# Placing the moving and the stationary operand of 1296 matmuls at equal addresses modulo 512 bytes

## The chip, the core and the metric

The kernel runs on one core of one Trainium2 chip. The metric is device time in microseconds. Three runs of the kernel before gave 567.34, 567.60 and 567.75 us; the median, 567.6 us, is the time before. In the text, PE is TensorE, DVE is VectorE, ACT is ScalarE, POOL is GpSimd and SP is SyncE.

## The reference

Three layers follow each other: attention with a window, a mixture of experts, and a gated layer. The last one takes most of the time, and the change is made there.

```
x = attention(q, k, v)        # 2 batches, 8 heads, 768 positions, 64 wide -> 1536 tokens x 512
x = moe(x, w_gate, w_output_gate, w1, w2)       # 8 experts, 512 -> 1024 -> 512, one per token
gate = 1 / (1 + exp(-(x @ w_gate)))             # 1536 x 512 times 512 x 1536
val  = x @ w_val                                # the same shape
out  = (gate * val) @ w_out                     # 1536 x 1536 times 1536 x 512
```

The weights of the last layer come as 64-bit floats, and the kernel turns them to 32 bits itself.

## The kernel before, in words

**Split operands.** A product that must be better than one pass of the type float32r is made of three. Each operand x is split in a high part, `hi` (line 131, on ACT), and the rest, `lo` (line 134, on DVE or POOL): high by high, high by low and low by high are added in one PSUM bank.

**The experts (before 254 us).** Seven items of up to 256 tokens of one expert are computed. `item_A` (line 652) makes the hidden layer: the weights are the stationary operand (128x128), the tokens the moving one (256 columns). `item_B` (line 661) makes the output: the hidden layer `hh`, `hl` is stationary, the weights `w2h`, `w2l` move with 512 columns. All these tiles lie in the pools `mA2` and `mB`. A last, short item (lines 671 and 683) follows.

**Gate and value (254 to 457 us).** The tokens are transposed into `yb[b]`, three pairs (high and low) of tiles of 128 x 4 x 512, one pair for each block `b` of 512 tokens. `gate_val(f, b)` makes 12 matmuls for the gate in a PSUM bank of the tag A and 12 for the value in a bank of the tag B: four chunks `c` of the inner dimension by three products. Stationary is `wh` or `wl` (chunk c, 128x128, 512 bytes in each partition), moving is `yb[b]` (chunk c, 512 columns, 2048 bytes in each partition). ACT takes the sigmoid of the first bank (line 1145), DVE multiplies it with the second (line 1146, recorded at 137) into `gg`. The columns f run from 0 to 11, each with b = 0, 1, 2, except at the start, where f = 0 and 1 are mixed: (0,0), (1,0), (0,1), (0,2), (1,1), (1,2). Between the chunks DVE does the conversion of the next weights, seven operations each (lines 760 to 777), ACT and POOL split them.

**Output (457 to 558 us).** For each of 12 tiles of 128 tokens, 36 matmuls run (line 1176): `gs`, the split product of gate and value (128x128), is stationary; the split output weights move, 512 columns. These weights are written into the same tiles `yb`, which the tokens no longer need: `yb[0]` holds f = 0 to 3, `yb[1]` 4 to 7, `yb[2]` 8 to 11. DVE copies the bank out, POOL sends the rows with an indirect DMA (line 1179).

**What sets the order and the addresses.** The order is the order of the code on each engine. A tile's address is set by what was laid in the same side of the memory before it: pools on the left side count up from the low end in the order of the code, those on the right count down from the high end. `yb[0]` is the last tile but a few small ones in the pool `cp`, on the left; `wh` and `wl` lie in `wsp` and the four tiles `yr` in `yrp`, both on the right; `gs` lies in `d1`, on the right as well, below them.

The lines that the change and the prediction's steps touch are: the tiles of `cp` (163 to 182), the pools `yrp` and `wsp` (1046 to 1052), `gate_val` (1125 to 1146), `g_split` and `wo_split` (1110 to 1123), and the output loop (1169 to 1181).

Of the kernel before, what the change touches and what calls it, by code (L numbers as in the profile page):

```python
# [10 lines left out]
F32 = mybir.dt.float32  # L11
F32R = mybir.dt.float32r
# [96 lines left out]
def moe_kernel(tc, A, out):  # L109
# [4 lines left out]
    def pool(st, name, side=None, space=None):  # L114
        kw = dict(name=name, bufs=1, reuse_waits="tile")
        if side:
            kw["side"] = side
        if space is not None:
            kw["space"] = space
            kw.pop("reuse_waits")  # L120
        return st.enter_context(tc.tile_pool(**kw))

    cp = pool(top, "cp", "left")
# [39 lines left out]
    x_t = dp.tile([S, DM], F32, name="x_t")  # L163
    y_c = dp.tile([NTOK + SLOT, XW], F32, name="y_c")

    ck = cp.tile([128, 128], F32, name="ck")
    ident = cp.tile([128, 128], F32, name="ident")
    ckb = cp.tile([128, CKB], BF16, name="ckb")
    wgo = cp.tile([128, 4, 16], F32, name="wgo")
    lg = cp.tile([128, NT, 16], F32, name="lg")  # L170
    OH = cp.tile([128, NT, 8], BF16, name="OH")
    cum = cp.tile([128, B, 2, 8], BF16, name="cum")
# [6 lines left out]
    gidx = cp.tile([128, 18, 2], I32, name="gidx")  # L179
    gix = cp.tile([128, 2], I32, name="gix")  # L180
    row_id = cp.tile([128, 12], I32, name="row_id")
    yb = [[cp.tile([128, 4, 512], F32R, name=f"yb0{k}") for k in range(2)]]
    tri, ones = ckb[:, 0:128], ckb[:, 128:256]
    count, token = ckb[:, 256:256 + SLOT], ckb[:, 256 + SLOT:256 + SLOT + 2 * TB].rearrange("p (t k) -> p t k", k=2)
    k8e, ke = ck[:, 0:8], ck[:, 16:24]
# [447 lines left out]
    def split2(p):  # L633
        s = slice(2 * p, 2 * p + 2)
        hi(w2h[:, s], w2r[:, s])
        lo(w2l[:, s], w2r[:, s], w2h[:, s])
# [9 lines left out]
    def item_A(f):  # L646
        hp = bank("A", 3)[:, 0:SLOT]
        s = slice(f * 128, f * 128 + 128)
        n = 0
        for c in range(4):  # L650
            for w, x in ((w1h, xTh), (w1h, xTl), (w1l, xTh)):
                PE.matmul(hp, w[:, c, s], x[:, c], start=n == 0, stop=n == 11)  # L652
                n += 1
        SC.activation(out=hh[:, f], in_=hp, func=AF.Relu)
        V.scalar_tensor_tensor(out=hl[:, f], in0=hp, scalar=0.0, in1=hh[:, f].bitcast(F32), op0=ALU.max, op1=ALU.subtract)  # L655
# [7 lines left out]
    def last_item(yp):  # L663

        t = slice(0, 128)
        ht = [w1r[:, q] for q in range(2)]

        def part(q, hp, cs_):
            for c in cs_:
                for n, (x, w) in enumerate(((xTh, w1h), (xTl, w1h), (xTh, w1l))):  # L670
                    PE.matmul(hp, x[:, c, t], w[:, c, q * 512:q * 512 + 512], start=c == 0 and n == 0, stop=c == 3 and n == 2)

        def turn(q):
            tp = bank("B", 2).rearrange("p (g c) -> p g c", g=4)
            for g_ in range(4):
                PE.transpose(tp[:, g_], ht[q][:, g_ * 128:g_ * 128 + 128], ident)
            s = slice(4 * q, 4 * q + 4)
            hi(hh[:, s, t], tp)
            lo(hl[:, s, t], tp, hh[:, s, t])

        def second(f):
            for n, (x, w) in enumerate(((hh, w2h), (hh, w2l), (hl, w2h))):
                PE.matmul(yp[0], x[:, f, t], w[:, f], start=f == 0 and n == 0, stop=f == 7 and n == 2)

        split2(1)
        hp = bank("A", 3)
        part(0, hp, range(4))
        SC.activation(out=ht[0][:, 0:512], in_=hp, func=AF.Relu)
        hp = bank("A", 3)
        part(1, hp, range(2))  # L690
        turn(0)
        part(1, hp, range(2, 4))
        split2(2)
        SC.activation(out=ht[1][:, 0:512], in_=hp, func=AF.Relu)
        for f in range(2):
            second(f)
        turn(1)
        split2(3)
        for f in range(2, 8):
            second(f)  # L700
# [52 lines left out]
    def ypsum(i):  # L753
        t = ps.tile([128, 2, 512], F32, tag="C", bufs=1, name=f"yp{i}")
        return t[:, 0], t[:, 1]
# [34 lines left out]
    wsp = {}  # L790
# [29 lines left out]
    def run(g, n=1):  # L820
        for _ in range(n):
            next(g, None)

    with tc.manual_schedule():
# [186 lines left out]
        for i in range(NSTAT):  # L1011
            if i == 3:
                last = nc.values_load(itab[0:1, 1, 15:16], engines=(ET.SP, ET.DVE), min_val=NSTAT - 1, max_val=MAXI - 1, skip_runtime_bounds_check_because=SKIP)
            if i == NSTAT - 1:
                yp = ypsum(i)
                last_item(yp)
                break
            if i:
                for f in range(8):
                    item_A(f)  # L1020
                    if f % 2 == 0:
                        split2(f // 2)
                    elif i > 1:
                        run(bg, 1)
                    if i == 1:
                        if f in (1, 3, 4, 5):
                            run(tb, 1)
                        if f == 5:
                            item_regs(2)
                            item_gather(2, gidx[:, 2])  # L1030
            if i < NSTAT - 1:
                load_w(reg["e", i + 1], reg["e", i + 1] != reg["e", i], range(8) if i else range(4, 8))
            yp = ypsum(i)
            for f in range(8):
                item_B(f, yp)
                if f % 2 == 0 and i < NSTAT - 1:
                    split1(f // 2)
                if f in (4, 5) and (f == 4 or i < NSTAT - 2):
                    item_T(i + 1, f - 4)
                if i and f in ((1, 2, 3) if i == 1 else (1, 2, 3, 6)):  # L1040
                    run(bg, 1)
                if not i and f == 0:
                    run(g, 9)
                    tail_st.close()

                    yr_st = ExitStack()
                    yrp = pool(yr_st, "yrp", "right")
                    yrt = [yrp.tile([128, XW], F32, name=f"yr{k}") for k in range(4)]
                    for t in yrt:
                        G.memset(t, 0.0)  # L1050
                    ws_st = ExitStack()
                    wsp_ = pool(ws_st, "wsp", "right")
                    cv_st = ExitStack()
                    cv = pool(cv_st, "cv", "right")

                    todo = [("w", f, k) for f in range(2) for k in range(2)]
                    bg = background(todo)
                    for k in todo[:3]:
                        load_raw(k)
                if not i and f in (1, 3, 7):  # L1060
                    run(tb, 1)
                if i == 5 and f in (0, 2, 3, 6):
                    t = (0, 2, 3, 6).index(f)
                    y_T(t)
                    load_y(t + 4, few)
                if i == 5 and f == 7:
                    split2(0)
            if i < NSTAT - 1:
                item_out(i, yp, reg["c", i] if i else 0)
            if 0 < i < NSTAT - 2:  # L1070
                if i + 2 == NSTAT - 1:
                    V.tensor_copy(gix, gidx[:, bass.ds(last, 1)].rearrange("p o h -> p (o h)"))
                item_gather(i + 2, gix if i + 2 == NSTAT - 1 else gidx[:, i + 2], halves=1 if i + 2 == NSTAT - 1 else 2)
            for k in (() if i == 0 else (3, 4) if i == 1 else (i + 3,)):
                more(k)

            if i == 4:
                n_items = nc.values_load(itab[0:1, 0, 15:16], min_val=0, max_val=MAXI - 1, skip_runtime_bounds_check_because=SKIP)
                few = n_items < NSTAT
                for t in range(4):  # L1080
                    load_y(t, few)
# [30 lines left out]
        def g_split(t):  # L1112
            for k in range(2):
                gs[t, k] = d1.tile([128, 2, 6, 128], F32R, tag="gs", bufs=3, name=f"gs{t}{k}")
                src = gg[:, 6 * k:6 * k + 6, t * 128:t * 128 + 128]
                hi(gs[t, k][:, 0], src)
                lo(gs[t, k][:, 1], src, gs[t, k][:, 0])
# [38 lines left out]
        for f in range(2, 12):  # L1156
            if f == 11:
                run(bg, 999)
                cv_st.close()
                d1_st = ExitStack()  # L1160
                d1 = pool(d1_st, "d1", "right")
            for b in range(3):
                gate_val(f, b)
                if f == 11:
                    if b == 0:
                        g_split(0)
                    for w in range(4 * b, 4 * b + 4):
                        wo_split(w, G if w % 2 else None)
        for t in range(12):
# [12 lines left out]
        y_st.close()  # L1182
        g_st.close()
        d1_st.close()
        ws_st.close()
        yr_st.close()
    top.close()


# [57 lines left out]
```

## Time and profile before

| | us |
|---|---|
| median of three runs | 567.6 |
| the profiled execution, its own time | 565.83 |
| its span, first to last instruction | 564.0 |
| PE busy (matmuls) | 542.9 |
| DVE busy | 386.8 |
| ACT busy | 213.7 |
| POOL busy | 124.8 |
| line 1136, first to last matmul's start | 254.1 to 457.4 |
| line 1176, first to last matmul's start | 457.7 to 557.4 |

A matmul of 512 columns is shown as 394 ns long, but the next one starts long before it ends, so the busy times of single matmuls overlap. What a matmul costs in a row of them is the distance between starts: a group of 12 in the chain of waits takes some 2.8 us, which is 232 ns each. The numbers in the prediction are such distances.

### The profile page before, as it was taken

Reading aid. Unit: us, or ns where it says so; the run is one execution under the profiler, and the core shown is the slowest. Engines: PE = TensorE matmul, PEld = TensorE weight load, DVE = VectorE, ACT = ScalarE, POOL = GpSimd, SP = SyncE. Lnnn points to the kernel's source line nnn. Section 1 sums busy time; section 2 is a strip of 40 time slices with the busy share of each in tenths; the row PEclk is TensorE's granted clock in tenths of the full one; section 3 lists DMA queues with packets and bytes.
Section 4 is the critical chain, followed back from the end, with each engine's and each line's share of the span. In section 5 each row is a group of like instructions: output and inputs, shape, how many; then the busy total and the mean of one; then the engine's idle time right before and its main releaser. Section 6 shows DMA issues by size and latency. Waiting matters only on the chain.

```text
span 564.0 us, 8978 instructions
## 1 busy us (share of the span) xinstructions
PE 542.9 (96%) x3236; PEld 458.9 (81%) x3236; DVE 386.8 (69%) x735; ACT 213.7 (38%) x391; POOL 124.8 (22%) x151
## 2 busy tenths in 40 slices
PE   8899989989999999989999999999999999999995
PEld 4688979878989989868888888888888888888884
DVE  4777677879777687853778899999987763323320
ACT  2866774654546555643221212212111442112110
POOL 3673044173101100000011111111111152212211
PEclk9989999999999999999999999999999999999998
DMA  8991465962478403216132323323322000001010
GB/s 326 414 408 39 149 245 179 382 247 74 133 268 268 160 24 108 76 57 206 38 100 87 101 87 112 112 76 112 111 76 76 1 1 37 20 37 38 19 38 37
DMA packets 31983, 71.62 MB, mean 127 GB/s; under 512 B 3056, under 2 KB 11712, under 8 KB 31936
## 3 DMA queue, kind: packets, MB, share of 16 engines
q1 hardware_dynamic: 28816, 60.96, 30.9%
q0 software_dynamic: 3120, 10.06, 5.2%
q8 instruction: 26, 0.43, 0.3%
q14 instruction: 21, 0.17, 0.1%
HBM read 72.53 MB, written 11.33 MB: 149 GB/s over the span
## 4 chain that ended last, share of the span: by engine, by line
PE 34%; issue 15%; POOL 5%; ACT 0%; POOLq 0%; DVE 0%; DVEq 0%; ACTq 0%
PE ps_A L1136 18%; PE ps_B L1136 15%; POOL out_dram L1179 3%; POOL yb L134 1%; PE ps_B L746 1%; POOLq L1243 0%; ACT yb L131 0%; ACT gs L131 0%; DVE yt L141 0%; DVE gg L137 0%; POOLq L1179 0%; POOL yt L706 0%; POOLq L1084 0%; DVEq L137 0%; POOLq L134 0%
## 5 line engine op out<-in xcount | busy, mean ns | idle before, releaser
L1136 PE MATMUL ps_A<-yb,wh 128*128 128x512 f32 x312 | 98.3, 396 | 2.0 <-DVE yt L141 2.0
L1176 PE MATMUL ps_A<-yb,gs 128*128 128x512 f32 x432 | 100.1, 394 | 0.0
L1176 PEld LDWEIGHTS ps_A<-yb,gs 128*128 128x128 f32 x432 | 81.4, 188 | 18.6
L1136 PE MATMUL ps_B<-yb,wh 128*128 128x512 f32 x264 | 82.7, 394 | 0.0
L1136 PEld LDWEIGHTS ps_A<-yb,wh 128*128 128x128 f32 x312 | 58.1, 189 | 15.2 <-issue 2.4
L1136 PE MATMUL ps_A<-yb,wl 128*128 128x512 f32 x156 | 61.5, 394 | 0.0
L1136 PEld LDWEIGHTS ps_B<-yb,wh 128*128 128x128 f32 x264 | 49.7, 188 | 11.1
L1145 ACT ACTIVATE sg<-ps_A 128x512 f32<-128x512 f32 x36 | 21.5, 596 | 97.0 <-PE ps_A L1136 87.2
L134 POOL TENSOR_TENSOR wl<-cvw,wh 128x512 fp32r<-128x512 f32 x20 | 26.4, 1320 | 141.3 <-ACT wh L131 128.4
L652 PE MATMUL ps_A<-xTh,w1h 128*128 128x256 f32 x192 | 54.8, 285 | 1.7 <-DVE hl L655 1.7
L652 PE MATMUL ps_A<-xTl,w1h 128*128 128x256 f32 x192 | 54.5, 284 | 1.5 <-DVE xTl L134 1.5
L652 PE MATMUL ps_A<-xTh,w1l 128*128 128x256 f32 x192 | 54.4, 283 | 0.0
L1136 PE MATMUL ps_B<-yb,wl 128*128 128x512 f32 x132 | 51.9, 393 | 0.0
L131 ACT ACTIVATE gs<-gg 128x768 fp32r<-128x768 f32 x24 | 20.3, 845 | 71.3 <-PE ps_A L1176 69.1
L134 DVE TENSOR_TENSOR gs<-gg,gs 128x768 fp32r<-128x768 f32 x24 | 23.0, 958 | 34.9 <-ACT gs L131 34.8
L143 DVE TENSOR_SCALAR cva<-cva 128x512 f32<-128x512 f32 x72 | 41.8, 581 | 1.9
L134 DVE TENSOR_TENSOR w2l<-w2r,w2h 128x1024 fp32r<-128x1024 f32 x28 | 34.2, 1226 | 10.2 <-ACT w2h L131 10.0
L661 PE MATMUL yp<-w2h,hh 128*128 128x512 f32 x96 | 39.0, 406 | 0.0
L652 PEld LDWEIGHTS ps_A<-xTh,w1h 128*128 128x128 f32 x192 | 36.8, 192 | 2.1 <-DVE hl L655 1.9
L652 PEld LDWEIGHTS ps_A<-xTl,w1h 128*128 128x128 f32 x192 | 36.9, 192 | 1.9 <-DVE xTl L134 1.8
L661 PE MATMUL yp<-w2h,hl 128*128 128x512 f32 x96 | 37.6, 391 | 0.0
L661 PE MATMUL yp<-w2l,hh 128*128 128x512 f32 x96 | 37.6, 391 | 0.0
(229 smaller groups left out, 966.7 us busy)
## 6 DMA issues: line engine op xcount, KB each, us to landing
w1r<-in_w_dram SPq DMA_DIRECT2D x28, 512.0 KB
w2r<-in_w_dram SPq DMA_DIRECT2D x28, 512.0 KB
raw<-in_wgv_dram SPq DMA_DIRECT2D x24, 512.0 KB
vt<-in_vv_dram SPq DMA_DIRECT2D x12, 520.0 KB
raw<-in_wo_dram SPq DMA_DIRECT2D x12, 512.0 KB
kg<-in_kg_dram SPq DMA_DIRECT2D x8, 496.0 KB
y_c<-yt SPq DMA_DIRECT2D x13, 256.5 KB
yr<-y_c SPq DMA_DIRECT2D x12, 256.5 KB
```

The lines of the kernel that those rows point to most:

```text
L131: SC.activation(out=o, in_=i, func=AF.Copy)
L134: (eng or V).tensor_tensor(out=o, in0=i, in1=h.bitcast(F32), op=ALU.subtract)
L143: V.tensor_scalar(out=o, in0=a, scalar1=s1, scalar2=s2, op0=op0, op1=op1)
L652: PE.matmul(hp, w[:, c, s], x[:, c], start=n == 0, stop=n == 11)
L661: PE.matmul(yp[h], x[:, f, s], w[:, f], start=f == 0 and n == 0, stop=f == 7 and n == 2)
L746: PE.transpose(tp[:, c], r[:, c * 128:c * 128 + 128], ident)
L1136: PE.matmul(pp, w[:, c], x[:, c], start=n == 0, stop=n == 11)
L1145: SC.activation(out=sg, in_=pp, func=AF.Sigmoid)
L1176: PE.matmul(po, g2[:, x, f % 6], yb[f // 4][w][:, f % 4], start=f == 0 and n == 0, stop=f == 11 and n == 2)
L1179: d = G.indirect_dma_start(out=out[:, :], out_offset=bass.IndirectOffsetOnAxis(ap=row_id[:, t:t + 1].bitcast(U32), axis=0), in_=ot, in_off ...
```

## The change

It moves tiles in the memory and adds one small tile that nothing reads or writes. The number of instructions, their engines and their order stay as they are on all engines.

```
+    wgo = cp.tile([128, 4, 16], F32, name="wgo")
+    yb = [[cp.tile([128, 4, 512], F32R, name=f"yb0{k}") for k in range(2)]]
     ck = cp.tile([128, 128], F32, name="ck")
...
-    wgo = cp.tile([128, 4, 16], F32, name="wgo")
...
-    yb = [[cp.tile([128, 4, 512], F32R, name=f"yb0{k}") for k in range(2)]]
...
+                    ws_st = ExitStack()
+                    wsp_ = pool(ws_st, "wsp", "right")
                     yr_st = ExitStack()
                     yrp = pool(yr_st, "yrp", "right")
...
-                    ws_st = ExitStack()
-                    wsp_ = pool(ws_st, "wsp", "right")
...
                         g_split(0)
+                        d1.tile([128, 96], F32, name="edge1")
...
+        yr_st.close()
         ws_st.close()
-        yr_st.close()
```

The addresses that follow, in bytes of a partition, as the built programs have them. A chunk of a moving tile is 2048 bytes, one of a stationary tile 512, so the remainder modulo 512 is the same for every chunk of a tile.

| tile | before | modulo 512 | after | modulo 512 |
|---|---|---|---|---|
| `yb[0]`, high and low | 20800, 28992 | 320 | 16768, 24960 | 384 |
| `yb[1]`, `yb[2]` | 138624 to 163200 | 384 | the same | 384 |
| `wh`, `wl`, eight buffers | 200448 to 214784 | 256 | 208768 to 223104 | 384 |
| `gs`, three buffers | 182016 to 194304 | 256 | 181632 to 193920 | 384 |
| `w2h`, `w2l` (line 661, moving) | 122368, 138752 | 0 | the same | 0 |
| `hh`, `hl` (line 661, stationary) | 155136, 163328 | 0 | the same | 0 |
| `ident` (moving in the transposes) | 17024 | 128 | 33664 | 384 |

The distance of moving less stationary operand, modulo 512, is thus 64 bytes for `yb[0]` and 128 bytes for `yb[1]` and `yb[2]` before, and 0 for all three after. The conversion buffers `raw`, `cva`, `cvb` and `cvw` and all tiles of the experts keep their addresses. `ident`, `ck`, `ckb`, `wgo` and the small tiles of `cp` move.

Since `yr` and `wsp` change places, other instructions are the first to write where the attention's tile `late` stood, and a wait for the DMAs that read `late` moves with them. On POOL, in the place where the first items end and `yr` is cleared, the difference is this (- is before, + the change; `DMASW` are the semaphores of POOL's own DMAs).

```order
 L443 DMA x_s<-late,posi 1536x520 [waits DMASW1_49]
-L1050 MEMSET yr_1636 128x520 [waits DMASW5_49,DMASW4_49,DMASW6_49,DMASW1_49,DMASW7_49,DMASW0_49,PE_49]
-L1050 MEMSET yr_1637 128x520
-L1050 MEMSET yr_1638 128x520
-L1050 MEMSET yr_1639 128x520 [waits PE_49,Activation_49]
+L1052 MEMSET yr_1639 128x520 [waits PE_49]
+L1052 MEMSET yr_1640 128x520
+L1052 MEMSET yr_1641 128x520
+L1052 MEMSET yr_1642 128x520
 L524 COPY o_es<-ck 128x8 [waits DMAHW7_49]
```

The memset of the first `yr` loses the wait for the scatters from `late`. It goes to POOL's next gather of rows (line 587), which stands behind five other instructions, to the first `wl` on DVE and to the second `wh` on ACT. The second `wl` on DVE, the fourth `wh` on ACT and the first load of `yr` on SP lose such a wait.

## Rows read from the trace of the kernel before

**Rows 1.** The page: span, and TensorE's granted clock in 40 slices.

```profile
span 564.0 us, 8978 instructions
...
PEclk9989999999999999999999999999999999999998
```

**Rows 2.** Windows: length, then PE, PEld, DVE, ACT, POOL busy, clock, DMA.

```profile
254.00:291.00 37.00, 36.90 (x176) 30.34 (x177) 22.48 (x38) 10.59 (x17) 3.32 (x6) 1.00 0.36 117
324.00:357.00 33.00, 33.00 (x144) 26.87 (x143) 30.67 (x50) 5.79 (x10) 5.33 (x4) 1.00 0.33 104
457.00:557.00 100.00, 100.00 (x434) 81.43 (x433) 31.60 (x36) 19.85 (x25) 21.31 (x13) 1.00 0.08 29
```

**Rows 3.** Chain that ended last: start us, us, engine tile line, instructions.

```profile
271.69 11.16 PE ps_A L1136 x48
...
307.88 2.76 PE ps_A L1136 x12
310.64 2.75 PE ps_B L1136 x12
313.39 2.79 PE ps_A L1136 x12
316.18 2.79 PE ps_B L1136 x12
318.97 2.78 PE ps_A L1136 x12
321.75 2.79 PE ps_B L1136 x12
```

**Rows 4.** Line 1176: duration min/median/max, first and last start.

```profile
L1176 PE MATMUL ps_A<-yb,gs x432: 387/393/405, 457.7 to 557.4; 128*128 128x512 f32 x144
```

**Rows 5.** Timeline of PE in one output tile: start us, us, operation.

```profile
466.00 2.70 PE L1176 MATMUL ps_A<-yb,gs 128*128 128x512 f32 x11
...
469.00 5.28 PE L1176 MATMUL ps_A<-yb,gs 128*128 128x512 f32 x22
```

**Rows 6.** Timeline of PE in `item_B` of the first item.

```profile
132.43 0.40 PE L661 MATMUL yp<-w2h,hh 128*128 128x512 f32 x1
...
133.59 0.39 PE L661 MATMUL yp<-w2h,hl 128*128 128x512 f32 x1
...
139.03 0.39 PE L661 MATMUL yp<-w2h,hl 128*128 128x512 f32 x1
```

**Rows 7.** Timeline of POOL: split of weights, then of output weights.

```profile
301.32 1.29 POOL L134 TENSOR_TENSOR wl<-cvw,wh 128x512 fp32r<-128x512 f32 x1 [4.64 <-ACT wh L131]
...
457.17 3.20 POOL L134 TENSOR_TENSOR yb<-wo,yb 128x512 fp32r<-128x512 f32 x2 [1.35 <-ACT yb L131]
```

**Rows 8.** Timeline of DVE: the first `wl`; then after the last gate and value.

```profile
161.10 0.68 DVE L134 TENSOR_TENSOR wl<-cvw,wh 128x512 fp32r<-128x512 f32 x1
...
458.54 2.39 DVE L134 TENSOR_TENSOR yb<-wo,yb 128x512 fp32r<-128x512 f32 x2
460.85 0.95 DVE L134 TENSOR_TENSOR gs<-gg,gs 128x768 fp32r<-128x768 f32 x1
```

**Rows 9.** Timeline of PE: four transposes of an item, four of `yr`.

```profile
141.27 0.60 PE L641 MATMUL ps_B<-ident,xg 128*128 128x128 f32 x4
...
254.90 0.60 PE L746 MATMUL ps_B<-ident,yr 128*128 128x128 f32 x4
```

**Rows 10.** Timeline of POOL where `yr` is cleared, and the next gathers.

```profile
121.21 0.98 POOL L443 DMA_INDIRECT x_s<-late,posi  x1 [0.30 <-DMA x_s<-late,posi]
124.18 1.95 POOL L1050 MEMSET yr<- 128x520 f32 x4 [1.98 <-PE ps_A L652]
...
135.13 1.54 POOL L587 DMA_INDIRECT xg<-x_s,gidx  x1 [7.51 <-ACT w1h L131]
```

**Rows 11.** Timeline after the last matmul.

```profile
557.81 0.69 DVE L1178 COPY yr<-ps_A 128x512 f32<-128x512 f32 x1 [7.64 <-PE ps_A L1176]
558.78 0.97 POOL L1179 DMA_INDIRECT out_dram<-yr,row_id  x1 [7.36 <-DVE yr L1178]
```

## The prediction

> **What bounds the kernel now.** I read the page first, for the span and the clock: 564.0 us, and a 9 in almost each of the 40 digits [rows 1]. Then the windows by stage: PE is busy 33.00 of 33.00 us in the middle of the gate and value stage and 100.00 of 100.00 in the output stage, at a granted clock of 1.00, its upper level of 2.4 GHz. DVE comes second, with 30.67 of 33.00 and 31.60 of 100.00 [rows 2]. Then the chain of waits, which in the gate and value stage is nothing but groups of 12 matmuls end to end [rows 3]. So the last 304 us of the kernel, from 254 us on, are a sum of distances between matmul starts, 864 at line 1136 and 432 at line 1176. No wait has to be removed; the only thing that can give is the distance.
>
> The groups of the chain are not of one length. Each column f makes six, for the token blocks 0, 1 and 2, bank A and bank B: 2.76 and 2.75 us for block 0, then 2.79, 2.79, 2.78, 2.79 for blocks 1 and 2, and the pattern repeats from column to column [rows 3]. By twelve: 5.51/24 = 229.6 ns for block 0, 11.15/48 = 232.3 ns for the others; 48 matmuls of other blocks, before the pattern begins, give 11.16/48 = 232.5. The instructions, the stationary tiles and the engines beside them are the same; what differs is the moving tile. By the addresses, block 0 moves from 64 bytes past the stationary operand modulo 512, blocks 1 and 2 from 128. In the output stage the same tiles move, and within one output tile 11 of the first 12 matmuls (`yb[0]`) take 2.70 us and 22 of the other 24 take 5.28. The last one's own 0.394 us [rows 4] goes off, and (2.70 - 0.394)/10 = 230.6 and (5.28 - 0.394)/21 = 232.7 ns are left [rows 5]. Over the stage the distance is (557.4 - 457.7)/431 = 231.3 ns [rows 4].
>
> The trace of before also holds distance zero: line 661, with the same types, 128x128 stationary and 512 columns moving, both operands on addresses that are multiples of 512. Its matmuls start at 132.43 behind the matmuls of line 652. The first five distances take (133.59 - 132.43)/5 = 232 ns, then it settles: the next 24 take (139.03 - 133.59)/24 = 226.7 ns [rows 6]. That is the value I take: 226.7 at 0 bytes, 229.6 at 64, 232.3 at 128.
>
> **The change part by part.** *Gate and value.* Of 864 matmuls, two groups of 12 (one of block 0, one of block 1) are cut in pieces of three by the transposes of `yr`. A cut stream is an unsettled stream, so I give them no gain. There remain 288 - 12 = 276 at 64 bytes and 576 - 12 = 564 at 128. 276 x (229.6 - 226.7) = 0.80 us and 564 x (232.3 - 226.7) = 3.16 us.
>
> *Output.* 432 x (231.3 - 226.7) = 1.99 us. The first stretch of each stream costs some five distances at 232 in place of 226.7, 0.03 us each for the few breaks: nothing.
>
> *Bounds of the distance.* The far end without a gain is what the trace has now, 0 us, and the unsettled distance of 232 ns at 0 bytes would even lose: 276 x 2.4 - 564 x 0.3 + 432 x 0.7 = 0.8 us. In the other direction no settled stretch of 512 columns in these rows is below 226.7; I allow 226, another 0.9 us. I take 226.7 because it is the only value that a long stretch shows for distance zero, and these stages are the longest unbroken streams of the kernel.
>
> *What hides the rest.* If PE goes faster by 2%, the others must keep up. A column's six groups take 16.66 us now, 72 x 226.7 = 16.32 then; DVE's work in it is 30.67/33.00 x 16.66 = 15.5 us [rows 2, 3], so DVE keeps 0.8 us a column. The low part of the next value weights is ready at 301.32 + 1.29 = 302.6 us, and the group that reads it starts at 310.64 [rows 3, 7]: 8 us of cover, of which a column takes 0.3. At the end of the stage the split output weights are done on POOL at 460.4 and on DVE at 460.9 [rows 7, 8]. The matmul that needs the low part of f = 10, which DVE makes last, is the 33rd of the first output tile, 457.7 + 32 x 0.2313 = 465.1; in the change 32 x 4.6 ns = 0.15 us earlier against it, of 4.2 us. If this cover were gone, PE would wait for at most the lateness of one split, once. The product `gs` of the second tile is begun at 460.85 and needed at 466.00 [rows 5, 8].
>
> *Other tiles that move.* `ident` goes from 128 to 384 modulo 512. Four transposes take 0.60 us at line 641, where the distance is 160 to 256 bytes, and 0.60 at line 746, where it is 288 to 384 [rows 9]. So 128 columns show no price for the distance, and I cost the 240 or so transposes at nothing; a nanosecond each, in either direction, would be 0.2 us. The wait for the scatters from `late` was over when the clearing of `yr` started at 124.18; its new holders start later, POOL's gather at 135.13 and DVE's first `wl` at 161.10 [rows 8, 10]. Behind the gather POOL has only small copies and the next gather. Nothing again, and up to the 2 us of the memsets in POOL's favour, where POOL is idle anyway. The end, copy and last indirect DMA after 557.8 [rows 11], stays as it is.
>
> *Sum.* 0.80 + 3.16 + 1.99 = 5.95, less 0.1 for the unsettled starts: 5.8 us. The profiled execution took 565.83 us, 1.8 more than its span, and would take 560.0. The median of the runs shown is 567.6, 1.8 above this execution; the same gain from it gives 561.8.
>
> **The rivals.** *It is not the address modulo 512 (no change).* Block 0's tiles lie low in the memory, far from the others, and line 661 has one pair of PSUM banks for an item where line 1136 takes another bank every 12 matmuls. Either could make the steps in the rows. Against it: the output stage keeps one bank for 36 matmuls, and its mixture costs what the gate's does, 231.3 against 16.66/72 = 231.4; and three distances stand in order of their size. The time would be 567.6. The Trainium skill speaks for this rival: its page "SBUF — State Buffer" (Who interferes with whom) gives PE two independent read ports, one for the moving operand and one for the weight load, and says that "PE and ACT never wait on anyone". By that rule no placement could change a distance; the 2.76 beside 2.79 in every column [rows 3] needs another cause then.
>
> *It settles only half.* Each group of 12 changes the bank, and the stream could fall back to the unsettled distance and settle again. Halfway, 229.4 ns, the gain is 276 x 0.2 + 564 x 2.9 + 432 x 1.9 = 2.5 us: 565.1. For it: the five slow distances at each new entry. Against it: between 133.59 and 139.03 the operands alternate between two moving and two stationary tiles and the stream stays settled [rows 6].
>
> *Equal addresses are the bad phase in a stream without pauses (slower).* At equal bytes both reads fall on the same place for the whole stream if they start together. Line 661 gets its phase from a stage of 256 columns before it; here it would come from the gate's own start, and the stationary tile begins at 384, not at 0. The slow distances at line 661 are this state. Decisive is a mean of 231.4 + 1.1/1.272 = 232.3 ns over the 1272 uncut matmuls, from where it is 0.2% slower; at 234 it costs 1272 x 2.6 = 3.3 us: 570.9. Against it: in the rows the state dies out after five matmuls.
>
> That another engine becomes the bound is covered above; it could take away a part, never more.
>
> **How the numbers follow.** What a measurement of this kernel can tell from no change is about 0.2%, 1.1 us. Forecast, 561.8 (own range 560.8 to 563.5): 0.56. Half, to 566.4: 0.16. No change: 0.16. Slower: 0.12. So faster 0.72, same 0.16, slower 0.12. The range for 8 in 10 begins at 560.8, with 226 ns and a little, and takes in the half case and most of no change: 560.8 to 567.8.
>
> **What would show it.** The chain's groups of 12 at line 1136 all at 12 x 226.7 = 2.72 us, with no difference between block 0 and the others; the starts at line 1176 97.7 us from first to last in place of 99.7; line 661 as before; everything up to 254 us within some 0.3 us. Wrong would be: groups that still go 2.75 and 2.79 (the address isn't it), groups equal but above 2.78 (bad phase), or a PE that waits at line 1136 for `wl` or `wh`.

## The result

The changed kernel took 558.73 us (median of 4 runs, 556.17 to 559.40) against 567.67 us (4 runs, 567.34 to 567.85): a ratio of 0.9847, with an interval of 0.9814 to 0.9879. That is 8.9 us less, where 5.8 were forecast; the forecast time, 561.8, and the low end of its range, 560.8, lie above it.

The page of the changed kernel, its chain of waits (start us, us, engine tile line, instructions) and line 1177, which is line 1176 of before:

```profile
span 557.4 us, 8974 instructions
...
PEclk9989999999999999998999999999999999999999
```

```profile
300.96 2.72 PE ps_A L1136 x12
303.68 2.72 PE ps_B L1136 x12
306.40 2.72 PE ps_A L1136 x12
309.12 2.72 PE ps_B L1136 x12
311.84 2.72 PE ps_A L1136 x12
314.56 2.72 PE ps_B L1136 x12
```

```profile
L1177 PE MATMUL ps_A<-yb,gs x432: 388/389/389, 453.1 to 550.8; 128*128 128x512 f32 x144
```

All groups of 12 take 2.72 us, 226.7 ns a matmul, whichever token block moves; before they went 2.76, 2.75, 2.79, 2.79, 2.78, 2.79 [rows 3]. The output stage takes 550.8 - 453.1 = 97.7 us where it took 99.7 [rows 4]. This part came as forecast, to the digit.

Two things did not. First, the gate stage begins 2.2 us earlier, at 251.87 us in place of 254.10. Three more rows of the kernel before show where that lies. They are from the timeline of POOL, DVE and PE (start us, us, operation, in brackets the idle time before it and what ended it), and the clearing of `yr` stands ahead of them, in [rows 10]:

```profile
126.32 0.31 POOL L524 COPY o_es<-cs 128x8 f32<-128x8 f32 x2
...
126.67 0.92 DVE L137 TENSOR_TENSOR o_lf<-o_le,o_es 128x728 f32<-128x728 f32 x1 [2.44 <-POOL o_es L524]
...
127.97 0.39 PE L652 MATMUL ps_A<-xTh,w1h 128*128 128x256 f32 x1 [1.66 <-DVE hl L655]
```

and after, the clearing with them; the matmul on PE has no idle time there, so that it stands in a row of matmuls 0.12 us apart and is not shown:

```profile
121.93 1.99 POOL L1052 MEMSET yr<- 128x520 f32 x4
...
124.12 0.31 POOL L524 COPY o_es<-cs 128x8 f32<-128x8 f32 x2
...
124.46 0.92 DVE L137 TENSOR_TENSOR o_lf<-o_le,o_es 128x728 f32<-128x728 f32 x1 [0.47 <-POOL o_es L524]
```

Before, the clearing of `yr` waited 1.98 us; behind it on POOL stood three small copies into `o_es`; for these waited DVE, with the table's `o_lf`, for 2.44 us; behind that stood `hl` on DVE; and for this waited PE. After, `yr` no longer lies where `late` was, the clearing starts at once, and the whole chain is gone.

Not all of the 2.2 us is this wait. Here are the matmul of line 652 that ends PE's last idle time ahead of the clearing and the first matmul of the gate stage, first in the kernel before, then in the changed one:

```profile
118.97 0.39 PE L652 MATMUL ps_A<-xTl,w1h 128*128 128x256 f32 x1 [1.46 <-DVE xTl L134]
...
254.10 0.73 PE L1136 MATMUL ps_A<-yb,wh 128*128 128x512 f32 x2 [1.99 <-DVE yt L141]
```

```profile
118.73 0.39 PE L652 MATMUL ps_A<-xTl,w1h 128*128 128x256 f32 x1 [1.46 <-DVE xTl L134]
...
251.87 0.73 PE L1136 MATMUL ps_A<-yb,wh 128*128 128x512 f32 x2 [1.99 <-DVE yt L141]
```

0.24 us are there ahead of the clearing, so they are not from the wait. From this matmul to the gate stage it is 135.13 us before and 133.14 after: the wait is 2.0 us.

Second, in this profiled execution something was given back. Windows of the changed kernel at the start of the gate stage (length, busy us of PE, PEld, DVE, ACT, POOL, granted clock, DMA share, GB/s):

```profile
230.00:252.00 22.00, 19.74 (x96) 15.53 (x95) 13.38 (x16) 10.86 (x15) 0.66 (x5) 1.00 0.20 62
252.00:256.50 4.50, 4.50 (x17) 3.74 (x18) 1.29 (x2) 1.20 (x2) 0.00 (x0) 0.62 0.39 120
256.50:290.00 33.50, 33.50 (x161) 27.82 (x160) 21.29 (x36) 9.45 (x15) 3.36 (x6) 1.00 0.36 113
```

PE had stood idle for 2.0 us ahead of the gate stage, as it did before, and this time the granted clock went to its lower level, 1.2 GHz, for a few us: 0.62 on the mean of that window. The stage took 453.1 - 251.9 = 201.2 us; without such a fall it takes 199.6 (below).

### The profile page after: what moved, and what is told of

It is laid out like the page before. It is cut to its first block, busy times and chain, and to the rows that moved or that the text cites. A ratio compares the mean times of both kernels' runs of the same rounds, so it can differ in the third digit from the quotient of the medians.

```text
span 557.4 us, 8974 instructions
## 1 busy us (share of the span) xinstructions
PE 536.9 (96%) x3236; PEld 457.5 (82%) x3236; DVE 385.8 (69%) x735; ACT 214.1 (38%) x391; POOL 126.7 (23%) x151
## 4 chain that ended last, share of the span: by engine, by line
PE 34%; issue 14%; POOL 5%; ACT 0%; POOLq 0%; DVE 0%; DVEq 0%; ACTq 0%
PE ps_A L1136 18%; PE ps_B L1136 15%; POOL out_dram L1180 3%; POOL yb L134 2%; PE ps_B L746 1%; POOLq L1244 0%; ACT yb L131 0%; ACT gs L131 0%; DVE yt L141 0%; DVE gg L137 0%; POOLq L1180 0%; POOL yt L706 0%; POOLq L1084 0%; DVEq L137 0%; POOLq L134 0%
## 5 line engine op out<-in xcount | busy, mean ns | idle before, releaser
L1136 PE MATMUL ps_A<-yb,wh 128*128 128x512 f32 x312 | 97.7, 394 | 2.0 <-DVE yt L141 2.0
L1177 PE MATMUL ps_A<-yb,gs 128*128 128x512 f32 x432 | 98.1, 389 | 0.0
L1136 PE MATMUL ps_B<-yb,wh 128*128 128x512 f32 x264 | 81.3, 389 | 0.0
L143 DVE TENSOR_SCALAR cva<-cva 128x512 f32<-128x512 f32 x72 | 43.3, 602 | 1.9
L134 DVE TENSOR_TENSOR w1l<-w1r,w1h 128x1024 fp32r<-128x1024 f32 x28 | 34.1, 1221 | 4.2 <-ACT w1h L131 4.1
```

Of the source, the lines that this page charges most:

```text
L134: (eng or V).tensor_tensor(out=o, in0=i, in1=h.bitcast(F32), op=ALU.subtract)
L143: V.tensor_scalar(out=o, in0=a, scalar1=s1, scalar2=s2, op0=op0, op1=op1)
L1136: PE.matmul(pp, w[:, c], x[:, c], start=n == 0, stop=n == 11)
L1177: PE.matmul(po, g2[:, x, f % 6], yb[f // 4][w][:, f % 4], start=f == 0 and n == 0, stop=f == 11 and n == 2)
```

## The experiments

The questions were: how much is the distance, how much the wait that moved, and is it the distance modulo 512 at all? The ratios of the first four and of two later runs are each to runs of the kernel before on the same chip (medians 568.6 to 569.2 us on the three chips). Single runs of it there go from 566.1 to 574.5 us, for the most part in step with the mean granted clock of the run; on the chip of the first four, 0.996 at 566.7, 0.994 at 566.4 to 567.6, 0.988 at 570.1 to 571.4, 0.979 at 574.3. So a median says less than the times of the stages in the traces, or runs at one clock.

**Distance alone: `addr_only`.** The pools keep the old order; small unused tiles bring all operands to 128 modulo 512.

```
+    yb = [[cp.tile([128, 4, 512], F32R, ...)]]     # first tile of cp
+    wgo = cp.tile([128, 4, 16], F32, name="wgo")
...
+                    yrp.tile([128, 32], F32, name="pad0")
...
+        yp_.tile([128, 64], F32, name="pad1")
```

> The kernel before with its pools in their old order, but with yb, wh, wl and gs all at 128 modulo 512 (distance 0 everywhere); the clearing of yr keeps its wait for the scatters from late. Theory (two causes): groups of 12 at line 1136 take 2.72 us, line 1176 97.7 us from first to last start, and PE still waits 1.9 us at 126 us for hl; 5.8 us less than before, 561.9, if TensorE's clock stays up at the start of the gate stage, 563.5 if it falls there. Rival (the distance gave all 8.9 us): 558.8, and no wait at 126 us. Rival (only the absolute place at 384 is good): no gain, 567.6.

562.49 us, ratio 0.9893 (0.9839 to 0.9946): 6.1 us less, with 3.1 to 9.2 in the interval, which by itself would not exclude the 8.9 of the rival. The trace does. In the chain:

```profile
313.65 2.72 PE ps_A L1139 x12
316.37 2.72 PE ps_B L1139 x12
```

and in the timeline of DVE and PE:

```profile
127.98 0.92 DVE L137 TENSOR_TENSOR o_lf<-o_le,o_es 128x728 f32<-128x728 f32 x1 [3.78 <-POOL o_es L524]
...
129.29 0.39 PE L652 MATMUL ps_A<-xTh,w1h 128*128 128x256 f32 x1 [3.00 <-DVE hl L655]
```

The groups take 2.72 us, the gate stage 199.6 us and the output stage 97.7, and the stall of PE is there, even longer. The first is the distance, the second is not. Since the operands stood at 128 here and at 384 in the changed kernel, it is the distance that counts and not the place. In this trace the clearing's own row names what it waited for:

```profile
125.50 1.95 POOL L1051 MEMSET yr<- 128x520 f32 x4 [3.31 <-DMA x_s<-late,posi]
```

**Pools swapped, distance 128: `swap_only`.** The changed kernel with 128 bytes more in `wsp`.

```
                         d1.tile([128, 96], F32, name="edge1")
+                        wsp_.tile([128, 32], F32, name="pad1")
```

> The changed kernel with 128 bytes of unused tile at the end of wsp, which puts wh, wl and gs at 256 modulo 512 and yb at 384: distance 128 in all 1296 matmuls; the pools keep the changed order. Theory (two causes): line 1136 in groups of 2.79 us, line 1176 some 0.4 us slower than before, and the wait of 1.9 us at 126 us gone: 2.2 us less, 0.8 us + 0.4 us more for the matmuls that had 64 bytes, so 566.6, and 1.6 more in runs whose clock falls at the start of the gate. Rival (all gain from the distance): 568.8.

566.91 us, ratio 0.9975 (0.9942 to 1.0009): by itself this is not clear of no change. A group in the chain, of block 0 as of the others:

```profile
309.81 2.79 PE ps_A L1136 x12
```

and DVE's `o_lf` in the timeline:

```profile
128.60 0.92 DVE L137 TENSOR_TENSOR o_lf<-o_le,o_es 128x728 f32<-128x728 f32 x1 [0.47 <-POOL o_es L524]
```

DVE waits for 0.47 us in place of 2.44, and no stall of PE stands behind it. But of the 2.0 us more than half goes back: the groups of block 0 are now at 128 bytes too, which makes the gate stage 0.8 us longer than before (204.4 us), and the output stage takes 100.2 us, 0.4 more. That leaves 0.8 us, too little for this comparison. `o_lf` comes 4.1 us later here than in the changed kernel. 2.5 of it are there at the first matmul of line 652 (93.70 us in place of 91.17), behind a window with a lower clock:

```profile
20.00:40.00 20.00, 17.68 (x159) 16.14 (x159) 11.82 (x27) 11.96 (x30) 15.61 (x31) 0.74 1.03 409
```

There it is 0.74, and 0.91 in the profiles of the kernel before and of the changed one. The other 1.6 us are an idle time of PE at line 415, 2.23 us long in place of 0.62. Both lie ahead of all that differs; why the second is longer stays open.

**The wait alone: `memset_late`.** The kernel before, its addresses untouched, with the four clearings issued behind the copies.

```
-                    for t in yrt:
-                        G.memset(t, 0.0)
...
                 if not i and f in (1, 3, 7):
                     run(tb, 1)
+                if not i and f == 7:
+                    for t in yrt:
+                        G.memset(t, 0.0)
```

> The kernel before, addresses and distances unchanged, with the four clearings of yr issued on POOL behind the copies into o_es and not ahead of them. Theory: the copies no longer stand behind a wait for the scatters, DVE's product o_lf starts 2.4 us earlier, hl is in time, PE's wait of 1.94 us at 126 us is gone; 2.0 us less than before, 565.6. Rival (the wait at 126 us is something else's, or the time is given back before 254 us): 567.6.

565.22 us, ratio 0.9933 (0.9902 to 0.9965): 2.0 to 5.6 us less, 3.4 between the medians. PE's stall is gone, the groups are as before, and the clearing still waits, now with nobody behind it:

```profile
123.86 1.96 POOL L1062 MEMSET yr<- 128x520 f32 x4 [1.12 <-DMA x_s<-late,posi]
...
123.89 0.92 DVE L137 TENSOR_TENSOR o_lf<-o_le,o_es 128x728 f32<-128x728 f32 x1 [0.46 <-DVE o_le L137]
```

So the two causes are separate, and either is to be had without the other. From the matmul behind the idle time of 1.46 us, at 118.17 us here, to the gate stage at 251.21 it is 133.04 us, as in the changed kernel, 2.1 less than before. In `addr_only` the same stretch took 136.37 us (118.96 to 255.33): there the clearing waited 3.31 us in place of 1.98 and PE 3.00 in place of 1.66. So the wait is not of one length, 2.0 us in one profiled execution and 3.3 in the other. At one clock, 0.994, the two runs at 565.15 and 565.20 us stand against five of the kernel before at 566.42 to 567.62, which is 1.2 to 2.5 us. The interval of the ratio holds these; how long the wait is on the average was not measured.

**The idle time ahead of the gate stage: `warm_gap`.** The changed kernel with seven matmuls whose result is not read.

```
+        fill = bank("M", 1)
+        for _ in range(7):
+            PE.matmul(fill, ones, ckb[:, 0:512], start=True, stop=True)
         with tc.For_i(NSTAT - 1, n_items, 1) as it:
```

> The changed kernel with seven matmuls of 512 bf16 columns, whose result nobody reads, on PE in its idle time ahead of the loop at 250 us. Theory: the granted clock fell to its half for 3.4 us after PE had stood idle for 2.0 us, at a cost of 1.6 us, in some executions; kept busy, PE keeps the upper level at 250 us in all executions, and all runs are near the fastest of the changed kernel, 556.2 to 557, with a smaller spread than 556.2 to 559.4. Rival (the spread has another cause): 558.7 with the same spread. If the seven outlast the idle time, up to 0.5 us more.

561.22 us, 559.89 to 562.73, ratio 0.9867 (0.9815 to 0.9920), where 556.2 to 557 was expected; the changed kernel, beside runs of another chip, has 0.9825 (below). In its profile the clock stays up and the gate stage takes 199.6 us. But the seven did not fill the idle time; they stand ahead of it.

```profile
250.56 1.46 PE L1085 MATMUL ps_M<-ckb 128*128 128x512 bf16 x6
...
253.96 0.74 PE L1139 MATMUL ps_A<-yb,wh 128*128 128x512 f32 x2 [1.94 <-DVE yt L141]
```

PE's idle time is still 1.94 us, and from the matmul behind the 1.46 us to the gate stage it is 134.6 us, 1.5 more than in the changed kernel. Had PE waited there for other engines' work, its idle time would have become shorter. I read it as the passage through the loop, which begins when PE's own work is done; no run here takes the loop out. My expectation that the seven would fill it was wrong, and one execution without a fall of the clock does not show that the seven prevent it.

**Other distances: three scans.** Unused tiles between the `yb` tiles and in `d1` give each block its own distance, two or three at each line.

```
+        yp_.tile([128, 64], F32, name="pad1")       # scan_a: yb[1] at 256
...
+        yp_.tile([128, 48], F32, name="pad2")       # scan_a: yb[2] at 448
...
-                        d1.tile([128, 96], F32, name="edge1")
+                        d1.tile([128, 104], F32, name="edge1")
```

> The changed kernel with unused tiles between the yb tiles: at line 1136 the distances are 0 (block 0), 256 (block 1) and 448 bytes (block 2), at line 1176 they are 32 (yb[0]), 288 (yb[1]) and 480 (yb[2]). Theory (the distance modulo 512 sets the step, 0 is best): block 0 in 12 x 226.7 = 2.72 us, the others longer, 2.75 to 2.85 us; the output stage over 98.5 us. Rival (a distance modulo 256 or modulo 128 decides): block 1 at 2.72 us as well, and block 2 (448 = 3 x 128 + 64) as 64 bytes did, 2.755. Rival (only moving ahead by up to half of 512 costs): blocks 448 and 480 at 2.72.

> As the scan before it, with the distances 0, 32 and 192 bytes at line 1136 and 96, 128 and 288 bytes at line 1176. Theory: 32 bytes between 226.7 and 229.6 ns, 96 between 229.6 and 232.3, 128 as in the kernel before, 232.3, and 192 above it if the price grows with the distance. Rival (a few good places, no order): 192 or 288 at 226.7, or 32 at 232.

> As the two scans before it, with the distances 0, 320 and 384 bytes at line 1136 and 64, 384 and 448 bytes at line 1176. In the two scans 0 and 256 took 226.7 ns and 32, 96, 128, 192, 288, 448 and 480 took 232.4 to 233.6. Theory (the distance counts modulo 256, and 0 and 64 alone are better than the rest): block 1 (320 = 256 + 64) in groups of 2.755 us as 64 bytes had before, block 2 (384) in 2.79 to 2.80 us. Rival (modulo 512, with 256 a second good place): 320 and 384 both at 2.79 to 2.80. Rival (the 229.5 ns of 64 bytes before were a mixture with the streams beside it): 64 at line 1176 and 320 at 232 to 233.

Pairs of groups of one block in the chain. In `scan_a` block 1 at 256 bytes, block 2 at 448, and block 0 of the next column at 0:

```profile
313.02 2.72 PE ps_A L1139 x12
315.74 2.72 PE ps_B L1139 x12
318.46 2.80 PE ps_A L1139 x12
321.26 2.80 PE ps_B L1139 x12
324.06 2.74 PE ps_A L1139 x12
326.80 2.72 PE ps_B L1139 x12
```

In `scan_b`, block 1 at 32 bytes and block 2 at 192:

```profile
314.84 2.80 PE ps_A L1139 x12
317.65 2.80 PE ps_B L1139 x12
320.45 2.80 PE ps_A L1139 x12
323.24 2.80 PE ps_B L1139 x12
```

and in `scan_c`, at 320 and at 384:

```profile
313.79 2.76 PE ps_A L1139 x12
316.55 2.75 PE ps_B L1139 x12
319.30 2.79 PE ps_A L1139 x12
322.09 2.79 PE ps_B L1139 x12
```

The mean distances between starts, worked out over all matmuls of a kind in the traces (one execution for each place of the tiles), without those at a transpose:

| bytes, modulo 256 | ns at line 1136 | ns in the output stage |
|---|---|---|
| 0 | 226.8 (0), 226.9 (256) | 226.7 (0) |
| 32 | 233.3 (32) | 233.6 (32), 233.3 (288) |
| 64 | 229.3 (64), 229.6 (320) | 229.6, 229.5 (64) |
| 96 | | 233.5 (96) |
| 128 | 232.4 (128), 232.7 (384) | 232.2, in `scan_b` 233.2 (128), 231.6 (384) |
| 192 | 233.2 (192), 233.3 (448) | 233.3 (448) |
| 224 | | 232.6 (480) |

The distance counts modulo 256, not 512: 256 is as good as 0, 320 costs what 64 does, 384 what 128 does. So the theory of `scan_a` was wrong, and its first rival right for 256 bytes but not for 448. And it is not a slope, as the theory of `scan_b` had it: of the places tried 0 is the one good one, 64 is halfway, and all others cost 5 to 7 ns on a matmul of 512 columns. The two values of 128 in the output stage, 1 ns apart, show that the distance is not all that counts; what else does stays open. The executions took 564.99, 568.32 and 565.60 us, in one run each.

**The changed kernel again, and both at once.** `after_again` is the changed kernel; `combo` is the changed kernel with the clearings moved as in `memset_late`.

> The changed kernel unaltered, to stand beside the other runs of this chip. Theory (distance 5.8 us, wait 2.0 to 3.4 us, clock up to 1.6 us back in some executions): ratio to before 0.983 to 0.987, line 1136 settled at 12 x 226.7 = 2.72 us per group and 97.7 us for line 1176 as in the first profile; in the profile either a fall of the clock at 250 us and a gate stage of 201.2 us, or no fall and 199.6. Rival (the 8.9 us of the first runs were partly chance): ratio 0.9898, the 5.8 us alone.

> The changed kernel, with the clearings of yr behind the copies into o_es as well. Theory: in the changed kernel the clearing waits for nothing any more and PE has no stall at 124 to 126 us, so nothing is left to gain there: ratio to before 0.981 to 0.986, as the changed kernel itself. Rival (the clearing still delays DVE's o_lf by 0.5 us and PE with it): 0.5 us less than the changed kernel.

559.67 us, ratio 0.9825 (0.9781 to 0.9869), which leaves out the rival's 0.9898, and 559.52 us, ratio 0.9845 (0.9811 to 0.9878). Within these intervals nothing is gained by doing both, as the clearing of the changed kernel waits for nothing. No version here is clearly better than the changed one. The windows at the gate's start show `combo` without the fall of the clock:

```profile
253.50:258.00 4.50, 4.36 (x26) 3.66 (x27) 1.93 (x4) 1.79 (x3) 0.00 (x0) 1.00 0.46 125
```

Its gate stage, from its first start to the first start of the output stage, took 453.27 - 253.64 = 199.6 us:

```profile
253.64 0.73 PE L1137 MATMUL ps_A<-yb,wh 128*128 128x512 f32 x2 [1.99 <-DVE yt L141]
...
453.27 4.92 PE L1178 MATMUL ps_A<-yb,gs 128*128 128x512 f32 x21
```

That of `after_again` took 201.2 us, with a fall of the clock to 0.79 on the mean of this window:

```profile
250.00:258.00 8.00, 6.01 (x25) 4.58 (x25) 2.73 (x4) 1.44 (x3) 0.84 (x6) 0.79 0.34 100
```

So a fall costs 1.6 us.

## Why the prediction was wrong

*The distance: right, in its size too.* The settled 226.7 ns of line 661 [rows 6] is what both stages took. The output stage gave 2.0 us as the sum had it; the gate stage, where the clock did not fall, went from 203.6 to 199.6 us, 4.0 us, which is 0.80 + 3.16. The two stages of `addr_only` took the same 199.6 and 97.7 us.

*The wait that moved: wrong.* This is the failed step. The prediction says of it "Nothing again, and up to the 2 us of the memsets in POOL's favour, where POOL is idle anyway". It followed the wait to its new holders and found them all late enough, which held. It did not ask who had been waiting behind the old holder. That POOL's clearing had waited 1.98 us stood in [rows 10], and behind it on the same engine stood the copies for which DVE waited 2.44 us, and PE 1.66 behind DVE. The term was put at nothing and measured 2.0 us. The forecast that all before 254 us would stay within some 0.3 us failed by it, and `memset_late` and `addr_only` show this on either side. The row also names PE as what ended the wait; the clearing waits for several semaphores, and the row of `addr_only` names the scatters.

*The rest.* Of the 8.9 us between the medians, 5.95 us are the distance and 2.0 us the wait, by the traces. The remaining 1.0 us is within the interval of the ratio (6.9 to 10.5 us) and I found no cause for it. Between the two profiled executions the account closes: the spans differ by 564.0 - 557.4 = 6.6 us, which is 2.2 ahead of the gate stage and 5.95 of distance, less 1.6 for the fall. That the changed kernel's profiled execution, at 559.40 us, came within 0.6 us of the 560.0 that the sum has for it is luck: the wait that it left out and the fall of the clock nearly cancel. And the step from there to the median, 1.8 us above the profiled execution, did not carry over: the changed kernel's median is 0.7 below its own. The fall of the clock makes 1.6 us between one execution and the next of the same kernel; the changed kernel's shortest run, 556.17 us, is the one with the highest mean clock, 0.999, beside 0.993 to 0.995 at 558.26 to 559.40. How often it falls at this place in each kernel was not counted.

*The rivals.* That the address is not the cause is refuted by `addr_only` and the scans. "It settles only half" and the bad phase did not come: the stream stays at 226.7 ns across all changes of the bank. The reading that "three distances stand in order of their size" was right for the three and wrong as a rule: 32 bytes cost more than 64. The Trainium skill's page "SBUF — State Buffer" (Who interferes with whom) calls PE's two read ports independent, and the prediction's first rival took from this that placement cannot matter. That reading does not fit what was measured: with the same instructions, 2.72 us a group at 0 and 256 bytes, 2.80 at 32 and 192. Where in the chip the time goes, at the ports or elsewhere, no run here shows.

## What to carry to other kernels

In a stream of weight loads and matmuls of 512 columns in float32r, put moving and stationary operands at equal addresses modulo 256 bytes; here it was worth 1.2 to 2.9% of such a stream and cost the order of some allocations and an unused tile of 384 bytes. Other types were not tried, nor other numbers of columns beside the transposes. When tiles change places, the waits between old and new owners of the memory change too: follow a wait not only to where it goes, but ask at its old place what stood queued behind it, engine by engine, until an engine on the path. And before an effect is forecast from the traces of other stages, see whether one of them already runs in the state that the change makes: the number found there was exact.

## What was not expected of the hardware

In the distances tried the price is a step and not a slope, and it is periodic in 256 bytes: 226.7 ns at 0, 229.5 at 64, 231.6 to 233.6 at 32, 96, 128, 192 and 224. Transposes of 128 columns showed no such price: the rows stand at 0.60 us for four at several distances [rows 9], and after the change as well.

```profile
256.54 0.60 PE L746 MATMUL ps_B<-ident,yr 128*128 128x128 f32 x4
```

An idle time of 2.0 us on PE was followed by a fall of the granted clock in 5 of 11 profiled executions, with the same instructions on either side in all but `warm_gap`: it fell in both profiles of the changed kernel and in those of the three scans, not in those of the kernel before, `addr_only`, `swap_only`, `memset_late`, `warm_gap` and `combo`. What decides it stays open.
